# Side work of the experts one instruction per tile, thirteen conversions beside the attention, rows loaded ahead of the stores of y

## The chip, the core and the metric

The kernel runs on one core of one Trainium2 chip. The metric is device time in microseconds (us), the median of several executions. One execution was profiled on the hardware; all rows below come from that one.

The engines have short names: PE is TensorE (PEld its weight loads), DVE is VectorE, ACT is ScalarE, POOL is GpSimd and SP is SyncE, which issues most DMA transfers. Each engine works through its own queue in order; semaphores order the engines among each other.

## The reference

```python
scores = matmul(z, z.T) / S                  # B = 4, S = 3072, 64 wide
out = u * matmul(maximum(scores, 0) ** 2, v)  # 256 wide
x = out.reshape(B * S, 256)                   # 12288 tokens in one list
expert_idx = argmax(x @ w_gate, axis=1)       # 8 experts, capacity 384 each
h = maximum(disp @ w1[e], 0); y = h @ w2[e]   # 256 -> 1024 -> 256, scaled by the gate
h = y @ w_in; g = h * sigmoid(h)              # 256 -> 2048
result = g @ w_out                            # 2048 -> 256
```

An expert takes the first 384 tokens that choose it; tokens beyond that give zero rows. Tokens are attended in order until every expert is full, so that the kernel computes one whole batch of queries and 384 more, and branches to further code only if an expert still has room. Every product is done as three products of a head (fp32r) and a remainder, to keep the precision of float32.

## The kernel before, in words

**Attention.** Queries come in chunks: six of 512 and one of 384. A chunk goes over 24 key tiles of 128. One tick of the stream `st` is one tile: `scores` (two matmuls into a ps_s bank, relu on ACT, square on DVE), `square` of the tile before (head `ah` on ACT, remainder `al` on DVE) and `values` of the tile three before (six matmuls). Everything else is put into ticks with `st.at(t, f)`, and within a tick it stands in the order in which it was put there: loads and splits of z and v, clearing of DRAM, each chunk's routing (`route`, nine ticks after a chunk's last tile, with small DVE instructions and four scatters on POOL), and the *conversions*.

**Conversions.** w_in and w_out come as 64-bit floats. A `Convert` turns 512 columns into head and remainder, in seven steps: ACT makes two scaled copies (L199, L200), DVE does bit operations (L202, L205, L207, L210), ACT copies the head, and a product, a subtraction and an addition follow (L214, L215, L217), on POOL in the attention and on DVE in a late one. There are 16. The first `CV_N` are spread over the attention's free ticks (`free`, from `CV_A` to `TL + CV_B`, from the `CV_OFF`-th tick behind a chunk's end on); the words are loaded five ticks ahead. The rest are *late*: they are done beside the experts.

**Experts.** Eight units follow, one expert each with 384 tokens. Unit 0 runs at the end of the attention's stream, then the branch (L929), then units 1 to 7. `inward(i, tick)` does unit i: `hidden` for eight tiles (6 matmuls each into one of four ps_a banks, relu on ACT, remainder on DVE, L614), with this unit's w2 split beside the first four (head on ACT, remainder on POOL, L563), then `expert_out` (twice 24 matmuls into ps_s, a copy, a store of y), with the next unit's w1 split, its transposes and `split_x` (L601 on ACT, L602 on DVE) beside it. `tick` is called behind every tile of `hidden` and at eight places of `expert_out`. SP loads, in the program's order: the next expert's index (`look_up`), w1, the next unit's rows `xg` from `disp` (L584, `load`), w2, and the two stores of y (L631).

**Side work.** Beside units 1 to 6 each tick takes the next step of `work`: the late conversions, and then `Blocks.steps`, which makes four sums of blocks of w_in in two halves (`put` is a head on ACT, then a remainder on DVE). The words of a late conversion have one tile (`ut`), and the next are loaded inside the conversion before. What is left of `work` is drained ahead of unit 7.

**The end.** `quad` and `Pair` do w_in, the sigmoid and w_out in blocks, TensorE bound, to the end of the kernel.

Of the kernel before, what the change touches and what calls it, by code (L numbers as in the profile page):

```python
# [11 lines left out]
I32 = mybir.dt.int32  # L12
# [8 lines left out]
P = 128  # L21


def raw(ap):
    return ap.bitcast(F32)
# [3 lines left out]
def attention_moe_swish_kernel(  # L29
# [16 lines left out]
    E, _, F = w1.shape  # L46
# [9 lines left out]
    NTM = QC // P  # L56
# [107 lines left out]


    CW = 512
    CV_OPS, CV_OFF, CV_A, CV_B = 7, 6, 26, -14
    CV_N = 10

    class Convert:  # L170
        def __init__(self, i, src, hi, lo):
            self.src, self.hi, self.lo = src, hi, lo
            self.late = i > CV_N
            self.rw = rawt[NR + i % 2].bitcast(I32)

        def load(self):
            if self.late:
                self.rw = pools["ut"].tile([P, 2 * CW], I32, tag="ut", name="words")
            rv = self.rw
            if len(self.hi.shape) == 3:  # L180
                rv = rv.rearrange("p (a b) -> p a b", a=self.hi.shape[1])
            nc.sync.dma_start(out=rv, in_=self.src)

        def steps(self):
            t0 = pools["cv"].tile([P, CW], I32, tag="c0", name="c0")
            t1 = pools["cv"].tile([P, CW], I32, tag="c1", name="c1")
            t2 = pools["cv"].tile([P, CW], F32, tag="c2", name="c2")
            w = self.rw.rearrange("p (n two) -> p n two", two=2)
            hw, lw = w[:, :, 1], w[:, :, 0].bitcast(U32)
            f0, f1, f2 = t0.bitcast(F32), t1.bitcast(F32), t2  # L190
            hi, lo = self.hi, self.lo
            g0, g1, g2 = f0, f1, f2
            if len(hi.shape) == 3:
                g0, g1, g2 = (x.rearrange("p (a b) -> p a b", a=hi.shape[1]) for x in (f0, f1, f2))
            V = nc.vector

            nc.scalar.activation(f0, w.bitcast(F32)[:, :, 1], AF.Abs, scale=2.0 ** -16)  # L199
            nc.scalar.mul(f2, lw, 2.0 ** -52)  # L200
            yield
            V.tensor_scalar(f0, f0, 2.0 ** -31, None, ALU.max)  # L202
            yield

            V.tensor_scalar(t0, t0, 4, 1, ALU.logical_shift_left, ALU.logical_shift_right)  # L205
            yield
            V.scalar_tensor_tensor(t0, hw, -0x80000000, t0, ALU.bitwise_and, ALU.bitwise_or)  # L207
            yield

            V.tensor_scalar(t1, t0, -0x800000, None, ALU.bitwise_and)  # L210
            head(nc.scalar, hi, g0)
            yield
            eng = V if self.late else nc.gpsimd
            eng.tensor_tensor(f1, f1, f2, op=ALU.mult)  # L214
            eng.tensor_sub(g0, g0, raw(hi))  # L215
            yield
            eng.tensor_tensor(lo, g0, g1, op=ALU.add)  # L217
            yield
# [422 lines left out]
    class Blocks:  # L641
# [15 lines left out]
        def steps(self):  # L657
            self.s3 = self.s3()
            V = nc.vector
            tmp = lambda n: pools["el"].tile([P, QC], F32, tag="a", name=n, bufs=3)  # L660

            def put(to, x):
                nc.scalar.copy(to[0], x)
                V.tensor_sub(to[1], x, raw(to[0]))

            for c in range(HF // 512):
                (a11h, a11l), (a12h, a12l), (a21h, a21l), (a22h, a22l) = (
                    [raw(x) for x in a[c]] for a in (self.a11, self.a12, self.a21, self.a22))
                x, y = tmp("x"), tmp("y")
                V.tensor_add(x, a21h, a22h)  # L670
                V.tensor_add(y, a21l, a22l)
                yield
                V.tensor_add(x, x, y)
                yield
                put(self.s1[c], x)
                yield
                z = tmp("z")
                V.tensor_sub(z, x, a11h)
                V.tensor_sub(z, z, a11l)
                yield  # L680
                put(self.s2[c], z)
                yield
                x, y = tmp("x"), tmp("y")
                V.tensor_sub(x, a11h, a21h)
                V.tensor_sub(y, a11l, a21l)
                yield
                V.tensor_add(x, x, y)
                yield
                put(self.s3[c], x)
                yield  # L690
                V.tensor_sub(y, a12h, z)
                V.tensor_add(y, y, a12l)
                yield
                put(self.s4[c], y)
                yield

    class Slots:

# [167 lines left out]
    def inward(i, tick, split=True):  # L866

        u = units[i]
        nxt = units[i + 1] if i + 1 < len(units) else None
        new = nxt and nxt.x is not u.x  # L870
        w2s = u.x.split_w2() if split and not u.s0 else []
        if new:
            nxt.x.look_up()
            nxt.x.load_w1()
        if nxt and i:
            nxt.load()
        for f in range(FT):
            u.hidden(f)
            if w2s:
                w2s.pop(0)()  # L880
            tick()
        if new:
            nxt.x.load_w2()
        side = nxt.x.split_w1() if new else []
        side = [[f] for f in side] + [[] for _ in range(FT - len(side))]
        if nxt and i:
            side[0] += [nxt.keep_ids, lambda: nxt.transposes(0)]
            side[1] += [lambda: nxt.split_x(0), lambda: nxt.transposes(1)]
            side[2] += [lambda: nxt.split_x(1)]

        def beside():
            for f in side.pop(0):
                f()
            tick()

        for d in range(NH):
            u.expert_out(d, beside)
# [2 lines left out]
    tc.mark_branch_hint_location("full", "LikelyTaken", engines=tuple(  # L900
        getattr(mybir.EngineType, n) for n in ("PE", "DVE", "Activation", "Pool", "SP")))
    if early:
        inward(0, st.tick, False)
    st.finish()
    if early:
        units[1].load()


    def unless_full(label=None):
# [59 lines left out]

    def work():  # L970

        if late:
            late[0].load()
        for n, cv in enumerate(late):
            for k, _ in enumerate(cv.steps()):
                if k == 4 and n + 1 < len(late):
                    late[n + 1].load()
                yield
        yield from blocks.steps()

    work = work()
# [6 lines left out]
    nc.scalar.activation(pools["sm"].tile([1, 1], F32, tag="m", name="m"), warm[0:1, 0:1], AF.Sigmoid)  # L988
    for i in range(first, len(units)):
        if i + 1 < len(units):  # L990
            inward(i, lambda: next(work, None))
        else:
            for _ in work:
                pass
# [2 lines left out]
            slots[0].load()  # L997
            n = [0]

            def prepare():  # L1000
                n[0] += 1
                if n[0] == FT:

                    raws = [wts.tile([P, GK * D], F32R, tag=f"rawt{k}", name=f"part{k}") for k in range(4)]
                    sets[0] = halves(raws) + halves(big[0:3])
                    slots[0].parts = sets[0]
                    prepare.it = slots[0].steps()
                if n[0] > FT:
                    for _ in range(2):
                        next(prepare.it, None)  # L1010
# [185 lines left out]
```

## Time and profile before

| what | value |
|---|---|
| median of 3 runs | 770.39 us (769.28 to 770.55) |
| the profiled execution | 770.27 us, its span 768.2 us |
| attention and unit 0 | from 0 to 336.4 us of the span |
| branch and units 1 to 7 | from 336.4 to 498.5 us |
| the rest | from 498.5 to 768.2 us |

The span is the time from the first to the last instruction of the core. A row of a timeline begins with its start in the span and its duration; idle time ahead of it stands in brackets with the instruction that ended it. A row of windows gives a stretch, its length, the busy time (and the number of instructions) of PE, PEld, DVE, ACT and POOL, the granted clock of TensorE as a share of full speed, the busy share of the DMA engines and what they moved in GB/s.

### The profile page before, as it was taken

Reading aid. Unit: us, or ns where it says so; the run is one execution under the profiler, and the core shown is the slowest. Engines: PE = TensorE matmul, PEld = TensorE weight load, DVE = VectorE, ACT = ScalarE, POOL = GpSimd, SP = SyncE. Lnnn points to the kernel's source line nnn. Section 1 sums busy time; section 2 is a strip of 40 time slices with the busy share of each in tenths; the row PEclk is TensorE's granted clock in tenths of the full one; section 3 lists DMA queues with packets and bytes.
Section 4 is the critical chain, followed back from the end, with each engine's and each line's share of the span. In section 5 each row is a group of like instructions: output and inputs, shape, how many; then the busy total and the mean of one; then the engine's idle time right before and its main releaser. Section 6 shows DMA issues by size and latency. Waiting matters only on the chain.

```text
span 768.2 us, 11355 instructions
## 1 busy us (share of the span) xinstructions
PE 727.2 (95%) x3951; PEld 644.0 (84%) x3951; DVE 535.8 (70%) x964; ACT 499.2 (65%) x986; POOL 250.2 (33%) x237
## 2 busy tenths in 40 slices
PE   8999999999999999978878879989999999999995
PEld 6888887888888889978878879979999999999884
DVE  6778777787786867615887952578766876766770
ACT  6668777787777888735544455576566665565761
POOL 8622406233061882444563565200003100040004
PEclk9999999999999999989989899999999999999999
DMA  5815425052361423524641444121000000010001
GB/s 177 278 72 168 148 55 193 1 180 96 119 225 43 139 92 127 158 90 145 207 159 57 141 153 162 67 87 29 15 1 30 26 2 0 1 55 1 1 1 55
DMA packets 50668, 72.18 MB, mean 94 GB/s; under 512 B 3446, under 2 KB 38684, under 8 KB 50608
## 3 DMA queue, kind: packets, MB, share of 16 engines
q1 hardware_dynamic: 48160, 65.03, 26.6%
q0 software_dynamic: 2448, 6.39, 2.3%
q8 instruction: 32, 0.52, 0.3%
q14 instruction: 28, 0.23, 0.1%
HBM read 46.05 MB, written 25.77 MB: 93 GB/s over the span
## 4 chain that ended last, share of the span: by engine, by line
PE 39%; DVE 8%; ACT 3%; DMA 2%; issue 1%; SPq 0%; POOL 0%; POOLq 0%; ACTq 0%
PE ps_s L760 16%; PE ps_s L237 5%; PE ps_a L1029 5%; PE ps_a L1030 5%; PE ps_a L1031 4%; PE ps_a L237 3%; DMA words<-in_w_out 2%; DMA xg<-disp 1%; DVE c L215 1%; ACT big L1051 1%; DVE big L614 0%; DVE sg L1042 0%; PE ps_a L595 0%; POOL out L771 0%; DVE c L214 0%
## 5 line engine op out<-in xcount | busy, mean ns | idle before, releaser
L237 PE MATMUL ps_a<-ah,big 128*128 128x512 f32 (+1 forms) x672 | 183.0, 388 | 0.6 <-ACT ah L355 0.6
L237 PEld LDWEIGHTS ps_a<-ah,big 128*128 128x128 f32 x672 | 124.1, 188 | 21.5 <-POOL big L298 1.0
L342 ACT ACTIVATE r<-ps_s 128x512 f32<-128x512 f32 (+1 forms) x168 | 98.2, 585 | 57.3 <-PE ps_s L237 53.4
L356 DVE TENSOR_TENSOR al<-ps_s,ah 128x512 fp32r<-128x512 f32 (+1 forms) x168 | 111.6, 664 | 30.8 <-ACT ah L355 30.8
L347 DVE TENSOR_TENSOR ps_s<-ps_s,r 128x512 f32<-128x512 f32 (+1 forms) x132 | 89.4, 678 | 40.8 <-ACT r L342 40.2
L563 POOL TENSOR_TENSOR big<-rawt,big 128x512 fp32r<-128x512 f32 x64 | 88.6, 1406 | 77.2 <-ACT big L161 56.2
L760 PEld LDWEIGHTS ps_s<-wo,big 128*128 128x128 f32 x792 | 103.3, 190 | 7.7 <-ACT rows L768 2.7
L760 PE MATMUL ps_s<-wo,big 128*128 128x256 f32 x792 | 105.9, 283 | 1.8 <-ACT rows L768 1.8
L771 POOL DMA_INDIRECT out<-rows,ids x24 | 25.4, 1059 | 248.5 <-ACT rows L768 243.9
L237 PE MATMUL ps_s<-qt,kz 128*128 128x512 f32 (+1 forms) x336 | 104.8, 388 | 0.3 <-POOL kz L292 0.2
L237 PE MATMUL ps_a<-al,big 128*128 128x512 f32 (+1 forms) x336 | 101.3, 382 | 1.8 <-DVE al L356 1.7
L355 ACT CAST ah<-ps_s 128x512 fp32r<-128x512 f32 (+1 forms) x168 | 95.6, 569 | 3.3 <-DVE ps_s L347 3.1
L237 PE MATMUL ps_a<-qt,big 128*128 128x384 f32 x336 | 71.5, 373 | 18.4 <-DVE big L614 18.1
L237 PEld LDWEIGHTS ps_a<-qt,big 128*128 128x128 f32 x336 | 66.5, 213 | 22.1 <-DVE big L614 21.0
L237 PEld LDWEIGHTS ps_a<-al,big 128*128 128x128 f32 x336 | 62.6, 188 | 13.9 <-DVE al L356 2.6
L237 PEld LDWEIGHTS ps_s<-qt,kz 128*128 128x128 f32 x336 | 62.8, 188 | 11.9 <-POOL kz L292 0.7
L161 ACT CAST big<-rawt 128x512 fp32r<-128x512 f32 x86 | 51.6, 623 | 0.0
L460 POOL DMA_INDIRECT disp<-xr,idx x27 | 27.1, 1002 | 75.3 <-ACT ah L355 57.4
L1052 DVE TENSOR_TENSOR big<-sg,big 128x512 fp32r<-128x512 f32 x66 | 45.3, 688 | 7.1 <-ACT big L1051 5.9
L1042 DVE TENSOR_TENSOR sg<-ps_a,sg 128x512 f32<-128x512 f32 x72 | 48.0, 686 | 2.8 <-ACT sg L1041 0.7
L1051 ACT CAST big<-sg 128x512 fp32r<-128x512 f32 x66 | 41.0, 622 | 11.1 <-DVE sg L1042 11.1
L760 PEld LDWEIGHTS ps_s<-wo,late_c 128*128 128x128 f32 x348 | 45.9, 189 | 2.6
(227 smaller groups left out, 1249.8 us busy)
## 6 DMA issues: line engine op xcount, KB each, us to landing
rawt<-in_w SPq DMA_DIRECT2D x32, 512.0 KB, 4.6
out<-zero SPq DMA_DIRECT2D x16, 768.0 KB, 6.9
rawt<-in_v SPq DMA_DIRECT2D x11, 512.0 KB, 4.2
rawt<-in_w_in SPq DMA_DIRECT2D x8, 512.0 KB, 4.6
disp<-empty SPq DMA_DIRECT2D x6, 528.0 KB, 7.1
xg<-disp SPq DMA_DIRECT2D x8, 396.0 KB, 5.4
zr<-in_zT SPq DMA_DIRECT2D x12, 256.0 KB, 3.9
ut<-in_uT SPq DMA_DIRECT2D x6, 512.0 KB, 4.7
```

Of the source, the lines that this page charges most:

```text
L161: eng.copy(hi, x)
L237: nc.tensor.matmul(*a, **k)
L342: nc.scalar.activation(r[:, :Q], s[:, :Q], AF.Relu)
L347: nc.vector.tensor_mul(s[:, :Q], s[:, :Q], r[:, :Q])
L355: nc.scalar.copy(ah[:, :Q], a[:, :Q])
L356: nc.vector.tensor_sub(al[:, :Q], a[:, :Q], raw(ah[:, :Q]))
L563: nc.gpsimd.tensor_sub(ls[q][:, cs], rawt[r0 + q][:, cs], raw(hs[q][:, cs])))
L760: nc.tensor.matmul(o, lhsT=w[:, cs], rhs=wo[:, f, c:c + D], start=m not in self.seen, stop=last and n == 2, skip_group_check=True)
L1029: nc.tensor.matmul(ps, lhsT=ah, rhs=th, start=start, stop=False, skip_group_check=True)
L1042: nc.vector.tensor_mul(sg, src, sg)
L1051: nc.scalar.copy(gh, g)
L1052: nc.vector.tensor_sub(gl, g, raw(gh))
```

## The change

The late conversions become three: `CV_N` is 13, and their ticks run from 14 to `TL - 4`, from the ninth tick behind a chunk's end. Late words lie in two tiles by turns (`ut` and `xr`), two are loaded at the first step of the side work, and the load after next follows a whole conversion. Steps of the side work are cut to about one DVE instruction each, with `put` in two steps, and are called only behind tiles 5 to 7 of `hidden` and at seven of the eight places of `expert_out`. The next unit's rows are loaded ahead of w1, and unit 1's rows ahead of unit 0's stores of y instead of behind them.

```diff
-    CV_OPS, CV_OFF, CV_A, CV_B = 7, 6, 26, -14
-    CV_N = 10
+    CV_OPS, CV_OFF, CV_A, CV_B = 7, 9, 14, -4
+    CV_N = 13
...
-            self.late = i > CV_N
+            self.late, self.n = i > CV_N, i
...
             if self.late:
-                self.rw = pools["ut"].tile([P, 2 * CW], I32, tag="ut", name="words")
+                name, n = [("ut", 2 * CW), ("xr", NTM * ROW)][self.n % 2]
+                self.rw = pools[{"ut": "ut", "xr": "xr"}[name]].tile([P, n], I32, tag=name, name="words")[:, :2 * CW]
...
             eng.tensor_tensor(f1, f1, f2, op=ALU.mult)
+            if self.late:
+                yield
             eng.tensor_sub(g0, g0, raw(hi))
...
             def put(to, x):
                 nc.scalar.copy(to[0], x)
+                yield
                 V.tensor_sub(to[1], x, raw(to[0]))
+                yield
...
                 V.tensor_add(x, a21h, a22h)
+                yield
                 V.tensor_add(y, a21l, a22l)
                 yield
                 V.tensor_add(x, x, y)
-                yield
-                put(self.s1[c], x)
                 yield
                 z = tmp("z")
                 V.tensor_sub(z, x, a11h)
+                yield
+                yield from put(self.s1[c], x)
                 V.tensor_sub(z, z, a11l)
-                yield
-                put(self.s2[c], z)
                 yield
                 x, y = tmp("x"), tmp("y")
                 V.tensor_sub(x, a11h, a21h)
+                yield
+                yield from put(self.s2[c], z)
                 V.tensor_sub(y, a11l, a21l)
                 yield
                 V.tensor_add(x, x, y)
                 yield
-                put(self.s3[c], x)
-                yield
-                V.tensor_sub(y, a12h, z)
-                V.tensor_add(y, y, a12l)
-                yield
-                put(self.s4[c], y)
-                yield
+                V.tensor_sub(z, a12h, z)
+                yield
+                yield from put(self.s3[c], x)
+                V.tensor_add(z, z, a12l)
+                yield
+                yield from put(self.s4[c], z)
...
         if new:
             nxt.x.look_up()
-            nxt.x.load_w1()
         if nxt and i:
             nxt.load()
+        if new:
+            nxt.x.load_w1()
         for f in range(FT):
             u.hidden(f)
             if w2s:
                 w2s.pop(0)()
-            tick()
+            tick(f)
         if new:
             nxt.x.load_w2()
+        if early and not i:
+            nxt.load()
...
-            tick()
+            tick(2 * FT - 1 - len(side))
...
     if early:
-        inward(0, st.tick, False)
+        inward(0, lambda f: st.tick(), False)
     st.finish()
-    if early:
-        units[1].load()
...
-        if late:
-            late[0].load()
+        for cv in late[:2]:
+            cv.load()
         for n, cv in enumerate(late):
-            for k, _ in enumerate(cv.steps()):
-                if k == 4 and n + 1 < len(late):
-                    late[n + 1].load()
-                yield
+            for _ in cv.steps():
+                yield
+            if n + 2 < len(late):
+                late[n + 2].load()
         yield from blocks.steps()
...
-            inward(i, lambda: next(work, None))
+
+            inward(i, lambda f: next(work, None) if f > 4 and f != FT else None)
```

## Rows read from the trace of the kernel before

**Rows 1.** Waits of PE, 300 to 505 us: in total, times, longest.

```profile
PE ps_a L237 <- DVE big L614: 18.1, 8, 4.6
PE ps_a L595 <- SPq L929: 4.9, 1, 4.9
```

**Rows 2.** Windows: the branch, units 1, 4, 6 and 7, and all eight stretches.

```profile
336.39:342.77 6.38, 1.45 (x8) 1.15 (x7) 0.02 (x1) 0.96 (x2) 0.19 (x1) 0.68 0.33 97
342.77:366.42 23.65, 20.28 (x104) 19.73 (x104) 13.90 (x23) 13.77 (x28) 9.99 (x8) 0.87 0.45 151
...
414.88:442.34 27.46, 21.05 (x103) 20.25 (x103) 24.41 (x32) 12.05 (x25) 12.76 (x10) 0.88 0.30 99
...
464.36:481.86 17.50, 17.50 (x103) 17.18 (x103) 5.58 (x10) 9.95 (x20) 10.21 (x9) 1.00 0.50 166
481.86:498.53 16.67, 16.67 (x98) 16.67 (x97) 9.35 (x16) 9.72 (x19) 5.05 (x4) 1.00 0.22 76
sum 162.14, PE 137.40 PEld 131.28 DVE 103.72 ACT 82.39 POOL 75.24; mean PE 17.17 PEld 16.41 DVE 12.96 ACT 10.30 POOL 9.41
```

**Rows 3.** Timeline, unit 1: the first words and what follows them.

```profile
350.61 0.66 ACT L199 ACTIVATE c<-words 128x512 f32<-128x512 f32 x1 [4.43 <-DMA words<-in_w_out]
...
352.84 4.69 PE L237 MATMUL ps_a<-qt,big 128*128 128x384 f32 x18 [3.37 <-DVE big L614]
```

**Rows 4.** Timeline, start of unit 3.

```profile
390.35 1.77 DVE L215 TENSOR_TENSOR c<-c,wo 128x512 f32<-128x512 f32 x1
...
392.88 0.66 ACT L199 ACTIVATE c<-words 128x512 f32<-128x512 f32 x1 [3.10 <-DVE wo L217]
...
395.71 1.53 PE L237 MATMUL ps_a<-qt,big 128*128 128x384 f32 x6 [2.50 <-DVE big L614]
```

**Rows 5.** Groups by line, 340 to 500 us: first and last conversion line of seven.

```profile
L215 DVE TENSOR_TENSOR c<-c,wo 128x512 f32<-128x512 f32 x6 | 8.4, 1408 | 0.0
...
L202 DVE TENSOR_SCALAR c<-c 128x512 f32<-128x512 f32 x6 | 2.5, 422 | 1.7 <-ACT c L199 1.7
```

**Rows 6.** Timeline, unit 6, which has no side work.

```profile
464.36 8.48 PE L237 MATMUL ps_a<-qt,big 128*128 128x384 f32 x48
...
466.13 0.56 DVE L614 SCALAR_TENSOR_TENSOR big<-ps_a,big 128x384 fp32r<-128x384 f32 x1 [6.22 <-ACT big L613]
...
476.80 0.56 DVE L602 TENSOR_TENSOR qt<-ps_a,qt 128x384 fp32r<-128x384 f32 x1 [0.82 <-ACT qt L601]
```

**Rows 7.** Line L215, late conversions: ns, least, median and most.

```profile
L215 DVE TENSOR_TENSOR c<-c,wo x6: 679/1766/1784, 358.7 to 410.2; 128x512 f32<-128x512 f32 x6
```

**Rows 8.** Timeline at the branch.

```profile
337.60 0.39 SPq L584 DMA_DIRECT2D xg<-disp  x1
...
341.32 1.51 PE L595 MATMUL ps_a<-ident,xg 128*128 128x128 f32 x6 [4.93 <-SPq L929]
```

**Rows 9.** Line L929, the branch: first and last start on SP.

```profile
L929 SPq EVENT_SEMAPHORE  x9: 17/17/17, 339.2 to 341.2; - x9
```

**Rows 10.** DMA issues, 318 to 345 us: KB each, us to landing.

```profile
yT<-y SPq DMA_DIRECT2D x2, 192.0 KB, 2.0
```

**Rows 11.** Timeline, routing of chunk 1 beside chunk 2.

```profile
115.15 1.22 DVE L455 TENSOR_TENSOR sl<-sl,base 128x4 f32<-128x4 f32 x1
...
118.98 0.30 PEld L237 LDWEIGHTS ps_a<-al,big 128*128 128x128 f32 x2 [2.17 <-DVE al L356]
```

**Rows 12.** Timeline, end of chunk 0.

```profile
39.97 0.62 POOL L159 TENSOR_SCALAR qt<-zq 128x512 fp32r<-128x512 f32 x1 [3.36 <-DMA zq<-in_zT]
...
41.93 2.55 POOL L298 TENSOR_TENSOR big<-rawt,big 128x512 fp32r<-128x512 f32 x2
...
44.63 1.07 PE L237 MATMUL ps_a<-ah,big 128*128 128x512 f32 x4
```

**Rows 13.** Timeline of POOL: a conversion's product in the attention.

```profile
251.25 1.30 POOL L214 TENSOR_TENSOR c<-c,c 128x512 f32<-128x512 f32 x1
```

**Rows 14.** Windows of 10 us, columns as in rows 2.

```profile
30.00:40.00 10.00, 10.00 (x46) 8.29 (x45) 6.94 (x11) 7.60 (x15) 4.45 (x5) 1.00 1.08 357
```

More of the change, by code (lines that the diff above doesn't have):

```diff
@@ L998, in attention_moe_swish_kernel, with prepare @@
             n = [0]
-            def prepare():
+            def prepare(f):
                 n[0] += 1
```

## The prediction

> **What bounds the kernel now.** I read the waits of TensorE first. Between 300 and 505 us it waits for almost one thing only: `hidden` (L237, ps_a) waits for the DVE subtraction L614, 18.1 us in 8 waits, and once for the branch (L929), 4.9 us [rows 1]. So the attention is bound by TensorE itself, and the part where something is to be had is the seven expert units behind the branch. Second, the busy times by unit, cut where the 48 matmuls of `hidden` begin [rows 2]. Unit 6, without any side work, takes 17.50 us and TensorE is busy in all of them; unit 7 takes 16.67. Unit 1 takes 23.65, unit 4 takes 27.46. Units 1 to 7 together take 162.14 - 6.38 = 155.76 us. Seven clean ones would take 6 x 17.50 + 16.67 = 121.67. So **34.1 us** are stall, all of it in units 1 to 5, and DVE is busy there in 24.41 of 27.46 us in unit 4, against 5.58 of 17.50 in unit 6.
>
> Third, the order of time around two of the stalls. In unit 1 the first step of the side work sits behind tile 0: ACT's L199 stands 4.43 us waiting for the words of w_out, the relu of the next tile is queued behind it, and TensorE runs out of banks [rows 3]. In unit 3 the steps from the unit before still fill DVE: L215 takes 1.77 us, ACT waits 3.10 us for DVE before L199, and the subtraction of tile 0 that TensorE needs comes so late that it stands for 2.50 us [rows 4]. TensorE always stops after 24 matmuls, that is after four tiles, because ps_a has four banks.
>
> **The expert units.** The side work now is one DVE instruction per step, behind tiles 5 to 7 and seven of the eight places of the output: 10 steps per unit, 60 in units 1 to 6. The work is 3 conversions x 8 steps and 2 x 18 steps of the blocks, 60 as well, so nothing is left for the drain before unit 7. Three conversions leave. Six cost 39.6 us of DVE here (seven lines of six instructions, from 8.4 us for L215 down to 2.5 for L202) [rows 5], so three take 19.8. DVE in units 1 to 5 was 103.72 - 0.02 - 5.58 - 9.35 = 88.8 us, less 5 x 5.58 for the units' own work 60.9; 41.1 remain, spread over six units: 6.9 + 5.58 = 12.4 us in 17.5. The throughput fits.
>
> Then the latency, on the clean unit 6 [rows 6]. Its start is 464.36; the subtraction of tile 0 ends 2.3 us later, that of the second split_x 13.0 us later (476.80 + 0.56). Six steps follow on DVE before the next unit's tile 0. At the mean of a step, 41.1/49 = 0.84 us (3 x 7 + 2 x 14 = 49 of the 60 steps have a DVE instruction), five of them take 4.2 us and end at 17.2; TensorE needs tile 0's bank back only after four tiles, at 17.5 + 8.48/2 = 21.7. The cover is about 4 us; without it each microsecond of lateness costs one. The three steps behind tiles 5 to 7 delay hl of the last tiles, which the output reads last: tile 5's subtraction starts at 1.77 + 5 x 1.04 = 7.0, and even with a step of 1.78 us [rows 7] behind it and behind tile 6's, tile 7's ends at 7.0 + 3 x 0.56 + 2 x 1.78 = 12.2; it is wanted at 8.5 + 22 x 0.174 = 12.3. The ACT copies (`put`) now have a step between them and the subtraction, so DVE no longer stands for them. The first words are loaded at the first step, behind tile 5: SP reaches that load about where it does now, ACT about 6 us later, which covers the 4.43 us. With two tiles (ut, xr) the next words are there a conversion ahead. Nothing stands that I can see: 34.1 us go. From 0 to 16 us of stall may remain (the upper end is the second rival); I take 2, because the mean of a step is nearer to the undisturbed 0.68 than to 1.78.
>
> A rule that speaks against this. Steps of DVE that read SBUF meet GpSimd's L563: L215 takes from 0.68 to 1.78 us [rows 7]. The Trainium skill (SBUF — State Buffer, Who interferes with whom) says that a DVE instruction with two SBUF inputs and a GpSimd instruction that reads SBUF exclude each other for the whole instruction. By that rule every step that meets one could pay the full 1.78; the trace shows both ends, so it agrees. With each step at that price the sum would be rival 1's, with the mean it is the forecast's.
>
> **The branch.** The load of unit 1's rows (L584) is issued at 337.60, behind the last store of y, and TensorE starts at 341.32 [rows 8]. SP's semaphores behind the branch run from 339.2 to 341.2: it waits there for its own transfers [rows 9]. With the rows loaded before the stores only the last yT is awaited, issued at about 336.9 and landed 2.0 us later [rows 10]: 339.0, and I estimate 0.5 us for the rest of the semaphores. TensorE starts at 339.6, **1.7 us** earlier (bounds: 0, if the store is as late as the rows; 2.4, without its wait). It still restarts at the lower of its two levels: in unit 1 the mean clock was 0.87 [rows 2], so 0.13/0.5 x 23.65 = 6.1 us were at 1.2 GHz, in two spells. One of the two goes with the wait for the words; the other, 3 us at half speed, costs 1.5 us over the clean unit. Behind the branch the rows' load goes ahead of w1 on SP, so w1 lands 0.5 us later; it is wanted only in the output.
>
> **The attention.** 13 conversions instead of 10, 91 steps in 76 free tiles instead of 70 in 70: fifteen tiles get two. DVE and ACT have the room on average (three conversions are about 6 us each on either over 270 us). Two places change.
> (a) At 115 us small DVE instructions of the routing meet a conversion on GpSimd (L455: 1.22 us) and TensorE's next weight load stands 2.17 us for `al` [rows 11]. The new offset 9 starts conversions after the routing: **-2.1 us** (0 to 2.2).
> (b) The first conversion now lies in tiles 14 to 19. On GpSimd its L214 and L215 stand between chunk 1's split (39.97, after a wait of 3.36 us for zq) and the split of the last v (41.93, 2.55 us for two halves), whose first half the second matmul of the run at 44.63 wants, at about 44.85 [rows 12]. It ends at 43.2 now. L214 and L215 add 2.6 us (1.30 each [rows 13]), and the second conversion's words, 512 KB, are queued ahead of zq while the transfers run at 357 GB/s [rows 14]: 1.5 us. 43.2 + 2.6 + 1.5 = 47.3: TensorE stands **2.5 us** (0 to 4).
> The last two conversions meet GpSimd's splits of batch 1 (250 to 288 us); I put 0.3 us there (0 to 3).
>
> **Sum.** Against the profiled execution's own 770.27 us (span 768.2; median of the runs 770.39, so the two can be used alike): -34.1 + 1.5 + 2.0 - 1.7 - 2.1 + 2.5 + 0.3 = -31.6, **738.7 us**. The other ends: without (b), without what remains and without the low clock 732; what follows is for the top.
>
> **Rivals.**
> 1. *The lock with GpSimd decides.* All steps pay 1.78: 8.2 DVE steps per unit are 14.6 + 5.6 = 20.2 us in 17.5, 2.7 us per unit, 16 in six, in place of my 2: 753 us. For: half of L215's instructions here take that long. Against: behind tiles 0 to 4 there are no steps, and that is when GpSimd splits w2; only the first steps of the output meet w1's splits. Chance 0.12.
> 2. *Attention gives some back.* (b) at 4 us, and the last conversion's four DVE steps at 1.78 in 7.2 us, 3 us of stall in place of 0.3: +4 to +6, 743 to 745. Chance 0.13.
> 3. *The doubled tiles stall.* If each of the fifteen tiles with two steps stops TensorE, at the 2.17 us of the stall at 119 us they cost 32.6 and the time is 771; from 31.6/15 = 2.1 us each on the kernel is slower than before (2.5: 776). Against: ten conversions cost one such stall now, and that one met the routing. Chance 0.03.
> 4. *The side work isn't done in its places*, is drained before unit 7 and costs there what it did: about 770. The count, 60 in 60, speaks against it: 0.01.
>
> **Chances.** The forecast, 733 to 742, has 0.71, the rivals 0.12, 0.13, 0.03 and 0.01. Range 732 to 752: it takes in rival 2 and most of what lies toward rival 1. About 0.2% is what a measurement of this kernel tells from no change: faster 0.96, same 0.01, slower 0.03.
>
> **What would show it.** Units 1 to 6 at 17.5 to 18.5 us from `hidden` to `hidden`; no wait of TensorE for L614; ACT's waits for words gone or in unit 1 alone; TensorE behind the branch at about 3.2 us after its last matmul instead of 4.9; no wait for `al` near 119 us; but a wait of TensorE for GpSimd's L298 near 45 us. It is wrong if L614 of tile 0 still comes over 4 us after the unit's start, which means that DVE isn't through with the last steps, or if new waits for `al` appear where tiles have two steps.

## The result and the profile after

The changed kernel takes **738.4 us** (median of 4 runs, 737.6 to 740.5), the kernel before on the same chip 770.0: ratio 0.959, 95% interval 0.957 to 0.962, so 4.1% faster. The prediction was 738.7, its range 732 to 752. The profiled execution took 737.7 us, its span is 735.9.

The waits of TensorE, whole span (in total, times, longest). The lines of the changed kernel have moved: `hidden` is L240 (L237 before), its DVE subtraction L617 (L614), the branch L935 (L929), a conversion's product, subtraction and addition L215, L218 and L220 (L214, L215, L217). Against [rows 1], L617 is gone from the list, the wait at the branch has halved, and two waits of the attention are new in it.

```profile
PE ps_a L598 <- SPq L935: 2.5, 1, 2.5
PE ps_a L240 <- POOL big L301: 2.4, 1, 2.4
...
PE ps_a L240 <- DVE al L359: 1.2, 1, 1.2
```

Busy time by unit, as in [rows 2]: the branch, then units 1, 4, 6 and 7.

```profile
338.50:342.89 4.39, 1.62 (x11) 1.08 (x10) 0.02 (x1) 1.01 (x3) 0.59 (x2) 1.00 0.15 55
342.89:362.21 19.32, 19.32 (x102) 18.89 (x103) 12.85 (x19) 12.76 (x25) 11.00 (x9) 0.91 0.63 207
396.96:414.33 17.37, 17.37 (x103) 17.25 (x103) 12.87 (x19) 11.44 (x23) 11.63 (x9) 1.00 0.52 169
431.70:449.08 17.38, 17.38 (x104) 17.26 (x103) 12.72 (x18) 11.05 (x23) 12.12 (x9) 1.00 0.50 168
449.08:465.74 16.66, 16.66 (x97) 16.66 (x97) 9.98 (x17) 10.16 (x20) 5.06 (x4) 1.00 0.23 76
```

Unit 4 went from 27.46 to 17.37 us, and DVE does 12.87 us in it where it did 24.41. TensorE is busy in all of a unit that has side work. Unit 1 is 2 us longer than the others, without a wait: its mean clock is 0.91.

The waits are only part of what went. By [rows 2], TensorE was busy for 137.40 - 1.45 = 135.95 of the 155.76 us of units 1 to 7 before, where clean units need 121.67. So 19.8 us of the 34.1 were idle time, and 14.3 us were matmuls that took longer, 13.7 of them in units 1 to 4, where the granted clock was 0.87, 0.92, 0.80 and 0.88. Unit 3 shows it:

```profile
388.88:414.88 26.00, 22.14 (x103) 20.68 (x103) 21.61 (x29) 13.16 (x28) 13.47 (x10) 0.80 0.47 157
```

In the changed kernel, where TensorE doesn't stop, it is 1.00 in units 2 to 7: the clock came back where the waits ended. (Not every wait had lowered it: unit 5 of before had waits and a clock of 1.00.)

The timeline of unit 4 shows how. The output's last steps still run on DVE, and two of them are long; but they are through before tile 0 of the next unit (414.33) needs its subtraction.

```profile
396.96 8.48 PE L240 MATMUL ps_a<-qt,big 128*128 128x384 f32 x48
398.78 0.56 DVE L617 SCALAR_TENSOR_TENSOR big<-ps_a,big 128x384 fp32r<-128x384 f32 x1 [0.56 <-ACT big L616]
...
410.89 1.67 DVE L693 TENSOR_TENSOR x<-x,y 128x512 f32<-128x512 f32 x1
412.48 1.78 DVE L695 TENSOR_TENSOR z<-wih,z 128x512 f32<-128x512 f32 x1
...
414.33 0.86 PE L240 MATMUL ps_a<-qt,big 128*128 128x384 f32 x4
```

Tile 0's L617 ends 2.4 us after the unit's start, as in the unit without side work [rows 6]; all 48 matmuls of `hidden` run without a gap.

In unit 1 the words' wait of [rows 3], 4.43 us, is 0.28:

```profile
344.94 1.00 SPq L183 DMA_DIRECT2D words<-in_w_out  x2
...
352.02 0.67 ACT L200 ACTIVATE c<-words 128x512 f32<-128x512 f32 x1 [0.28 <-DMA words<-in_w_out]
```

The attention gives a little back. At the end of chunk 0, beside [rows 12]:

```profile
43.24 1.49 POOL L215 TENSOR_TENSOR c<-c,c 128x512 f32<-128x512 f32 x1
...
44.23 0.61 PE L240 MATMUL ps_s<-qt,kz 128*128 128x512 f32 x2
...
44.70 1.54 POOL L218 TENSOR_TENSOR c<-c,wih 128x512 f32<-128x512 f32 x1
...
46.20 2.96 POOL L301 TENSOR_TENSOR big<-rawt,big 128x512 fp32r<-128x512 f32 x2
...
47.51 0.96 PE L240 MATMUL ps_a<-ah,big 128*128 128x512 f32 x3 [2.44 <-POOL big L301]
...
48.78 0.62 PE L240 MATMUL ps_s<-qt,kz 128*128 128x512 f32 x2
```

Two conversion instructions of GpSimd, L215 and L218, stand ahead of the split of the last v (L301), and TensorE waits for it: the tile that begins at 44.23 lasts 4.55 us where an undisturbed tile lasts 1.81 (2.74 more). The other place is at 265 to 272 us, in the second batch:

```profile
264.92 3.39 DVE L206 TENSOR_SCALAR c<-c 128x512 int32<-128x512 int32 x1
265.44 1.33 POOL L215 TENSOR_TENSOR c<-c,c 128x512 f32<-128x512 f32 x1
...
266.68 1.33 POOL L218 TENSOR_TENSOR c<-c,wo 128x512 f32<-128x512 f32 x1
...
268.23 0.69 DVE L350 TENSOR_TENSOR ps_s<-ps_s,r 128x512 f32<-128x512 f32 x1
...
269.56 0.73 PE L240 MATMUL ps_a<-al,big 128*128 128x512 f32 x2 [1.16 <-DVE al L359]
```

L206, a DVE step of a conversion whose median is 0.43 us, takes 3.39. The attention's own L350 stands behind it, `al` comes late, and two tiles last 3.25 and 2.25 us, 1.9 more than two clean ones. The wait for `al` near 119 us [rows 11] is gone.

The account below is worked out from the starts of matmuls in the two traces: the first and last tile of the attention, `hidden` of each unit, the first matmul of the part behind unit 7.

| stretch | before | after | change | predicted |
|---|---|---|---|---|
| attention, first tile to last tile | 307.92 | 310.69 | +2.8 | +0.7 |
| last tile to unit 1 | 30.44 | 27.74 | -2.7 | -1.7 |
| units 1 to 7 | 155.76 | 122.85 | -32.9 | -30.6 |
| from there to the end | 269.72 | 270.13 | +0.4 | 0 |

That is -32.4, of -32.6 between the two profiled executions (770.27 and 737.7); the rest lies outside the span.

### The profile page after: what moved, and what is told of

It is laid out like the page before. It is cut to its first block, busy times and chain, and to the rows that moved or that the text cites. A ratio compares the mean times of both kernels' runs of the same rounds, so it can differ in the third digit from the quotient of the medians.

```text
span 735.9 us, 11357 instructions
## 1 busy us (share of the span) xinstructions
PE 714.8 (97%) x3951; PEld 635.3 (86%) x3951; DVE 525.4 (71%) x955; ACT 502.8 (68%) x986; POOL 265.9 (36%) x246
## 4 chain that ended last, share of the span: by engine, by line
PE 48%; ACT 2%; DVE 1%; issue 1%; POOL 0%; POOLq 0%; ACTq 0%
PE ps_s L765 17%; PE ps_a L240 8%; PE ps_s L240 8%; PE ps_a L1036 5%; PE ps_a L1037 5%; PE ps_a L1038 5%; PE ps_a L598 1%; ACT big L1058 1%; DVE sg L1049 0%; POOL out L776 0%; DVE ps_a L1080 0%; ACT u L1079 0%; ACT u L1095 0%; ACT sg L1048 0%; ACT u L1105 0%
## 5 line engine op out<-in xcount | busy, mean ns | idle before, releaser
L240 PE MATMUL ps_a<-ah,big 128*128 128x512 f32 (+1 forms) x672 | 183.3, 389 | 3.0 <-POOL big L301 2.4
L240 PEld LDWEIGHTS ps_a<-ah,big 128*128 128x128 f32 x672 | 123.9, 188 | 24.5 <-POOL big L301 3.9
L350 DVE TENSOR_TENSOR ps_s<-ps_s,r 128x512 f32<-128x512 f32 (+1 forms) x132 | 89.3, 677 | 38.1 <-ACT r L345 36.6
L566 POOL TENSOR_TENSOR big<-rawt,big 128x512 fp32r<-128x512 f32 x64 | 90.3, 1436 | 43.0 <-ACT big L161 38.0
L240 PE MATMUL ps_s<-qt,kz 128*128 128x512 f32 (+1 forms) x336 | 105.3, 390 | 0.0
L240 PE MATMUL ps_a<-al,big 128*128 128x512 f32 (+1 forms) x336 | 101.5, 383 | 1.3 <-DVE al L359 1.2
L240 PEld LDWEIGHTS ps_a<-al,big 128*128 128x128 f32 x336 | 62.4, 188 | 13.9 <-DVE al L359 2.6
L240 PEld LDWEIGHTS ps_s<-qt,kz 128*128 128x128 f32 x336 | 63.0, 189 | 11.3 <-POOL kz L295 0.4
L240 PE MATMUL ps_a<-qt,big 128*128 128x384 f32 x336 | 61.3, 341 | 0.2 <-ACT qt L604 0.2
L240 PEld LDWEIGHTS ps_a<-qt,big 128*128 128x128 f32 x336 | 59.8, 192 | 0.8 <-ACT qt L604 0.5
L161 ACT CAST big<-rawt 128x512 fp32r<-128x512 f32 x86 | 51.4, 621 | 0.5 <-DMA rawt<-in_v 0.3
```

The source lines that it names most:

```text
L161: eng.copy(hi, x)
L240: nc.tensor.matmul(*a, **k)
L350: nc.vector.tensor_mul(s[:, :Q], s[:, :Q], r[:, :Q])
L566: nc.gpsimd.tensor_sub(ls[q][:, cs], rawt[r0 + q][:, cs], raw(hs[q][:, cs])))
```

## The experiments

No kernel here leaves out a part of the computation. The ratio is that to the kernel before on the same chip (three chips: medians 772.9, 772.75 and 770.5 us), and the stretches are those of the table above, from one profiled execution each. They are set side by side first, since several experiments are read against the same rows.

| kernel | ratio, 95% interval | attention | units 1 to 7 |
|---|---|---|---|
| before | 1 | 307.9 | 155.8 |
| changed | 0.959 (0.957 to 0.962) | 310.7 | 122.9 |
| changed_again | 0.960 (0.958 to 0.962) | 312.0 | 122.6 |
| rows_behind | 0.962 (0.960 to 0.965) | 313.5 | 122.4 |
| start_20 | 0.956 (0.954 to 0.958) | 310.8 | 122.9 |
| end_14 | 0.955 (0.953 to 0.957) | 309.7 | 121.9 |
| start_20_end_14 | 0.958 (0.956 to 0.960) | 312.8 | 122.6 |
| off_6 | 0.956 (0.954 to 0.958) | 310.2 | 122.2 |
| one_tile | 0.959 (0.957 to 0.961) | 312.3 | 122.7 |
| all_ticks | 0.973 (0.970 to 0.975) | 311.0 | 133.1 |
| coarse | 0.972 (0.968 to 0.975) | 313.7 | 129.9 |
| ten | 0.970 (0.968 to 0.972) | 306.8 | 134.9 |
| twelve_15 | 0.956 (0.955 to 0.958) | 309.3 | 123.6 |
| eleven_15 | 0.963 (0.961 to 0.965) | 308.6 | 130.5 |

Six of these executions (changed, changed_again, rows_behind, one_tile, all_ticks, coarse) place the conversions of the attention alike, and their attention still lasts from 310.7 to 313.7 us: the stall near 45 us costs 2.7 to 4.0 in them. A difference of a microsecond or two in that column says little alone.

**The rows behind the stores again.**

```diff
-        if early and not i:
-            nxt.load()
...
     st.finish()
+    if early:
+        units[1].load()
```

> The changed kernel, but unit 1's rows are loaded behind unit 0's stores of y again, as before the change. Theory (SP's wait for its own transfers sets the restart behind the branch): TensorE's wait there goes back from 2.5 us to 4.9 us, the time is 2.4 to 2.7 us above the changed kernel's 738.4, so about 741, and nothing else moves. Rival (the stores of y alone would hold the restart, the rows are hidden anyway): under 0.5 us.

The wait of TensorE:

```profile
PE ps_a L598 <- SPq L935: 4.9, 1, 4.9
```

It is that of before, 2.4 us more than in the changed kernel, and from the last tile to unit 1 the kernel takes 30.4 us, as before (27.7 in the changed one). By ratio it loses 0.3% (0.962 against 0.959), 2.3 us, with intervals that overlap. The gain at the branch comes from the rows' place.

**Where the first and the last conversion of the attention stand.** Three kernels with other bounds for the ticks:

```diff
-    CV_OPS, CV_OFF, CV_A, CV_B = 7, 9, 14, -4
+    CV_OPS, CV_OFF, CV_A, CV_B = 7, 9, 20, -4    # start_20
+    CV_OPS, CV_OFF, CV_A, CV_B = 7, 9, 14, -14   # end_14
+    CV_OPS, CV_OFF, CV_A, CV_B = 7, 9, 20, -14   # start_20_end_14
```

> The changed kernel with the first conversion at tile 20 instead of 14, so that its three GpSimd instructions stand behind the split of the last v; 91 steps lie in 70 tiles, 21 of them with two. Theory (the stall of 2.4 us near 45 us is GpSimd's order plus zq's delay): the wait for L301 falls to at most 0.3 us, since v's first half is done at about 44.6 and wanted at 44.9; the time falls by 2.4 to 2.7 us to about 735.8. Rival (tiles with two steps stall TensorE): new waits for the remainder al, no gain. Second rival (zq alone does it): over 1 us of the wait stays.

> The changed kernel with the last conversion ended at tile 120 instead of 139, out of the stretch in which GpSimd splits batch 1; 24 tiles have two steps. The first conversion's L215 and L218 come one tile earlier and can run while GpSimd waits for zq. Theory: the stall at 267 to 272 us (1.9 us over two tiles) goes; near 45 us only L220's 1.3 us stand ahead of the split of v, so that the wait there falls from 2.4 to about 1.2 us; together -3.0 us, about 735.4. Rival (the last stall comes from the splits and the routing alone, as the 0.3 us of the kernel before did): the stall stays, -1.2 us.

> Both shifts: conversions from tile 20 to tile 120 alone, 91 steps in 61 tiles, 30 of them with two steps. Theory (stalls come from where GpSimd's instructions meet the routing, the splits of v or the splits of batch 1, not from two steps in a tile): both stalls go, the attention takes what its matmuls take, -4.3 us, about 734.1. Rival (density stalls TensorE): thirty tiles with two steps cost more than the two stalls gave, 738 or above.

In start_20 the wait for L301 is gone; chunk 0 takes 41.59 us against 44.32 in the changed kernel and 41.58 before. So the first conversion made it. But the late stall grew to three tiles of 3.51, 3.69 and 2.67 us, and the profiled attention is no shorter. By ratio the kernel is 2.8 us faster than the changed one (0.956 against 0.959), about what was expected, but the intervals overlap and the profile doesn't show where. The timeline of start_20 there:

```profile
263.51 3.02 DVE L203 TENSOR_SCALAR c<-c 128x512 f32<-128x512 f32 x1
263.69 1.32 POOL L215 TENSOR_TENSOR c<-c,c 128x512 f32<-128x512 f32 x1
...
264.93 1.31 POOL L218 TENSOR_TENSOR c<-c,wo 128x512 f32<-128x512 f32 x1
...
267.79 0.73 PE L240 MATMUL ps_a<-al,big 128*128 128x512 f32 x2 [1.42 <-DVE al L359]
```

It is another line of the conversion that takes 3 us, L203, but again one that meets L215 and L218 of GpSimd. In end_14 the late stall is gone, as expected: no tile between 254 and 280 us lasts over 1.9 us. The wait for L301 is down to 0.9 us. New stalls of 0.5 to 1 us appear in tiles 115 and 121, and the profiled attention is 1.0 us shorter, not 3. By ratio it does gain what was expected, 3.6 us with intervals that don't overlap (0.9547 against 0.9594). The profiles place 1.0 us of it in the attention and 1.0 in unit 1, whose clock was 0.95; the rest they don't place. With both edits the two stalls are gone and tiles 25, 49, 73, 97 and 121 last 2.1 to 2.9 us: TensorE waits there for `ah` (3.1 us in 5 waits), since ACT has the conversion's copy L161 ahead of it, which stands 2.0 us for DVE's L208. So neither place need stall; thirteen conversions pushed into fewer tiles stall a little in many. That was the rival in the expectation, and it has the case: the attention takes 312.8 us, and by ratio the kernel is level with the changed one.

**The offset back at 6.**

```diff
-    CV_OPS, CV_OFF, CV_A, CV_B = 7, 9, 14, -4
+    CV_OPS, CV_OFF, CV_A, CV_B = 7, 6, 14, -4
```

> The changed kernel with conversions from the sixth tile behind a chunk's end on, as before the change: 91 steps in 91 tiles, none with two. Theory (GpSimd's conversion instructions slow the routing's small DVE instructions): stalls of about 2 us each where GpSimd's steps fall on the routing, at tiles 33 to 36 and 82 to 85, and the stall near 45 us gone, because the first conversion's GpSimd steps fall behind the split of v and the second's words behind zq; the stall near 268 us stays. Together +1 to +2 us. Rival (two steps in a tile make the stalls): with none left, all stalls go, -4 us.

The routing does meet a conversion again, in two places, and in one of them, in chunk 3, TensorE stalls (tile 84 lasts 3.56 us):

```profile
159.91 1.12 DVE L457 TENSOR_SCALAR dr<-sl 128x4 f32<-128x4 f32 x1
...
160.96 1.30 POOL L218 TENSOR_TENSOR c<-c,wih 128x512 f32<-128x512 f32 x1
161.06 1.21 DVE L458 TENSOR_TENSOR sl<-sl,base 128x4 f32<-128x4 f32 x1
...
162.33 1.29 POOL L220 TENSOR_TENSOR wil<-c,c 128x512 fp32r<-128x512 f32 x1
162.38 1.26 DVE L470 COPY count<-count 128x8 bf16<-128x8 bf16 x1
```

Three instructions on 128x4 or 128x8 elements take 1.1 to 1.3 us each; the same kind, undisturbed, takes 0.16 to 0.19 a moment before and after. This is the mechanism of term (a). But the whole isn't slower: with this offset the conversions miss the end of chunk 0 and nearly miss the late place, and by ratio it is level with start_20. It has another stall, in tile 146 at 280.8 us (3.43 us), where ACT stands 2.7 us for a transfer of v ahead of the copy that TensorE wants. The expectation that offset 9 is the better one, by 1 to 2 us, isn't borne out: it takes away one stall and brings two.

**The units: places, size and number of the steps.** First the steps behind all 16 places instead of ten:

```diff
-            inward(i, lambda f: next(work, None) if f > 4 and f != FT else None)
+            inward(i, lambda f: next(work, None))
```

> The changed kernel, but the side work is called at all sixteen places of a unit again instead of ten; it is then done in units 1 to 4. Theory (the five free tiles let DVE catch up before TensorE needs a bank): the first words are awaited at tile 0 of unit 1, 3 to 5 us; in units 2 to 4 sixteen steps of 0.84 us and 5.6 us of own work are 17.4 to 19 us of DVE in 17.4, so 0 to 1.5 us each; together 4 to 9 us above 738.4. Rival (the gain came from three conversions less and the second words' tile, the places are free): under 1 us. The waits of TensorE for L617 tell which.

Units 1 to 6 take 26.5, 17.9, 18.1, 19.2, 17.4 and 17.4 us. Unit 1 has most of it:

```profile
352.61 0.66 ACT L200 ACTIVATE c<-words 128x512 f32<-128x512 f32 x1 [5.76 <-DMA words<-in_w_out]
354.23 0.56 DVE L617 SCALAR_TENSOR_TENSOR big<-ps_a,big 128x384 fp32r<-128x384 f32 x1 [7.22 <-ACT big L616]
...
354.84 2.61 PE L240 MATMUL ps_a<-qt,big 128*128 128x384 f32 x7 [4.14 <-DVE big L617]
```

That is [rows 3] again. The words are no later than in the changed kernel; ACT reaches them 5.5 us earlier and stands, with the relus queued behind. Starting behind tile 5 covers this. The loss, 10.2 us in the units, is over the 4 to 9 expected. Units 2 to 4 lose 3.1 of it, as expected; unit 1 loses 7.2 where 3 to 5 were expected, 4.1 in the wait above and some 3 with its clock, which is 0.81 (0.91 in the changed kernel).

Next the steps of before, two DVE instructions or a copy and its remainder in one, in the new places (the conversion's product and subtraction in one step, `put` without a yield, the blocks' sums paired as before):

```diff
             eng.tensor_tensor(f1, f1, f2, op=ALU.mult)
-            if self.late:
-                yield
             eng.tensor_sub(g0, g0, raw(hi))
...
                 nc.scalar.copy(to[0], x)
-                yield
                 V.tensor_sub(to[1], x, raw(to[0]))
-                yield
```

> The changed kernel with the steps of the kernel before (two or three instructions in some, the head's copy and the remainder in one step): 41 steps instead of 60 at the same ten places per unit. Theory (short steps keep DVE from standing for ACT's copy and from running late): a unit's ten steps take about 11.3 us of DVE and some 2 us of waits for ACT, with 5.6 of its own over 17.4, so 1 to 2 us of stall in each of four units: 3 to 8 us above 738.4. Rival (only the places matter): under 1 us.

Units 1 to 3 take 18.7, 17.4 and 17.4 us; units 4 and 5, at whose starts the blocks' steps of the unit before are still running, 22.0 and 20.5. The start of unit 4 (line numbers are lower by two here):

```profile
404.10 1.80 DVE L693 TENSOR_TENSOR y<-y,wil 128x512 f32<-128x512 f32 x1
405.83 1.94 DVE L615 SCALAR_TENSOR_TENSOR big<-ps_a,big 128x384 fp32r<-128x384 f32 x4
406.43 5.68 PEld L238 LDWEIGHTS ps_a<-qt,big 128*128 128x128 f32 x24 [3.09 <-DVE big L615]
```

`hidden` begins at 399.33, and DVE is still in the block's steps: the first of them and the copy between keep it until 405.83, 6.5 us later, and then the subtractions come four at once. Small steps are needed, but only for the blocks' sums, which alternate with ACT. Two units pay 3.1 and 4.6 us where four were expected to pay 1 to 2 each; the 7.0 us together lie in the expected 3 to 8, the whole by ratio, 9 us, above it.

Third, ten conversions in the attention as before, six late ones (84 steps for 60 places):

```diff
-    CV_N = 13
+    CV_N = 10
```

> The changed kernel with ten conversions in the attention and six late ones: 48 + 36 = 84 steps for 60 places, so 24 steps are drained ahead of unit 7. Theory: 24 steps are 17 to 20 us of DVE, of which TensorE hides four tiles, 4.2 us: 13 to 16 us above, less up to 2 us of stall in the attention: 750 to 754. Rival (the number of late conversions matters little, since their DVE work was never the limit): under 3 us.

With thirteen conversions placed as in the changed kernel the attention takes 2.8 to 5.8 us more than before, in six profiled executions. With ten in the new places it is shorter than before, 306.8 against 307.9. But units 1 to 6 aren't disturbed either (18.2 us in unit 1, 17.4 in the others); what has no place is drained before unit 7, which takes 29.7 us instead of 16.7:

```profile
PE ps_a L240 <- DVE big L617: 10.8, 1, 10.8
```

The other 2.3 us of unit 7's 13.0 go with its clock, 0.83. By ratio the kernel is 8 us above the changed one, where 12 to 16 were expected: the attention is 3.9 us shorter than the changed kernel's, not up to 2.

Last, one tile for the words instead of two, loaded inside the conversion before, as it was:

```diff
-                name, n = [("ut", 2 * CW), ("xr", NTM * ROW)][self.n % 2]
+                name, n = ("ut", 2 * CW)
...
-        for cv in late[:2]:
-            cv.load()
+        if late:
+            late[0].load()
```

> The changed kernel with one tile for the late words, the next loaded inside the conversion before, as it was before the change; the places and the short steps stay. Theory (the wait for words mattered because it came ahead of tile 0's relu): ACT waits up to 2 us for the second and third words, at the last places of a unit, and TensorE sees nothing of it: within 0.5 us of the changed kernel. Rival (the second tile is what took away the waits): 3 us or more above, with TensorE waiting for L617 behind the words.

Units 1 to 6 take 19.1 and five times 17.4: the second tile isn't needed here.

**A version between.** If thirteen conversions are too many for the attention and ten too many for the units, twelve or eleven, with more places behind the tiles of `hidden` and all eight of the output, may do better:

```diff
-    CV_OPS, CV_OFF, CV_A, CV_B = 7, 9, 14, -4
-    CV_N = 13
+    CV_OPS, CV_OFF, CV_A, CV_B = 7, 9, 15, -4
+    CV_N = 12                                                      # eleven_15: 11
...
-            inward(i, lambda f: next(work, None) if f > 4 and f != FT else None)
+            inward(i, lambda f: next(work, None) if f > 3 else None)   # eleven_15: f > 2
```

> Twelve conversions beside the attention, from tile 15 on (84 steps in 75 tiles, nine with two), four late ones, and the side work called behind tiles 4 to 7 and at all eight places of the output: 32 + 36 = 68 steps in 72 places. Theory (stalls of the attention come from GpSimd's steps in bad places, and the units have room on DVE: 53 us of side work over six units and 5.6 us of own work are 14.4 in 17.4): no stall over 1 us in the attention, units 2 to 6 stay at 17.4 us; 3.5 to 4.5 us less than the changed kernel on the same chip. Rival (the units are full at ten steps): the units lengthen by 0.5 to 2 us each, no gain.

> Eleven conversions beside the attention from tile 15 on (77 steps in 75 tiles), five late ones, the side work behind tiles 3 to 7 and at all eight places of the output: 40 + 36 = 76 steps in 78 places. Theory: the attention runs without a stall, as it did with ten conversions; the units need about 60 us of side work, 15.5 of 17.4 us of DVE, so 0 to 1 us of stall each: between 4.5 us less and 1 us more than the changed kernel. Rival (three free tiles are too few): TensorE waits for L617 in each unit, over 1 us each.

> The changed kernel itself once more, so that the next kernels can be set beside it on one chip: 0.96 of the kernel before.

twelve_15 takes 736.65 us where the changed kernel takes 740.17 on the same chip, ratios 0.956 (0.955 to 0.958) and 0.960 (0.958 to 0.962): 3.5 us less, as expected. By ratio end_14, start_20 and off_6 are level with it. Its attention, 2.7 us shorter, has no stall at 265 to 272 us and none over about 1 us elsewhere; unit 1 is 1.3 us shorter, with a clock of 1.00 in this execution; units 2 to 4 pay 0.7 to 0.8 us each for four late conversions, as the rival in the expectation has it, but that doesn't take up the gain. Units 1 and 2:

```profile
341.37:359.13 17.76, 17.76 (x103) 17.33 (x103) 10.51 (x18) 12.25 (x25) 10.43 (x9) 1.00 0.60 206
359.13:377.31 18.18, 17.64 (x103) 17.20 (x103) 14.00 (x21) 11.79 (x25) 11.53 (x10) 1.00 0.62 213
```

eleven_15 is slower than the changed kernel, 742.5 us, by 0.3% with intervals that just touch: with steps behind tiles 3 and 4 as well, units 1 and 3 take 19.9 and 21.1, part of it at a clock of 0.91 and 0.92. Against twelve_15, one conversion fewer in the attention was worth 0.8 us there, and that conversion and the further place cost 6.9 in the units.

## Why the prediction was right, and where its terms were off

**The units' stall, -34.1, and what remains of it, +2.0.** Right in the sum, and a little too cautious: no wait of TensorE for L617 is left, so what remains is nothing, and the low clock in unit 1 costs 1.9 against the 17.4 of the others, with 1.5 forecast. A unit now takes 17.37 where the clean one took 17.50, 0.8 us in six. DVE has 12.9 us of work in unit 4, with 12.4 forecast from the average; by the same working a step takes 0.87 us at the mean (76.1 us of DVE in units 1 to 6, less 6 x 5.58, over 49), with 0.84 forecast. The 4 us of cover on which the sum rested are confirmed from the other side: in coarse DVE comes to tile 0 at 6.5 us, and TensorE stands 2.8 us at the start of units 4 and 5 each.

Two readings behind the term were too simple. It calls all 34.1 us stall, with the clock in unit 1 alone; but 14.3 of them were matmuls that took longer, nearly all in units 1 to 4 at a lower clock, and they went as the clock came back where the waits ended. And TensorE doesn't always stop after 24 matmuls: in unit 1 of before it did so after 30, since 18 are left in [rows 3].

The undo experiments give back 10 us (places), 7 (step size) and 12 (number of late conversions) of the units' 33, and none (second tile). They don't add up to 33, and needn't: DVE's lateness below the cover is free, so one part undone costs only what goes past it, and what the clock falls with it. No single one of these parts makes the gain. The order of the rows' load ahead of w1 in the units was not undone; no run shows its share.

**Rival 1, the lock with GpSimd.** It doesn't decide the units. Single steps do pay its price, 1.67 and 1.78 us for L693 and L695 above, which run beside GpSimd's splits (L566). The Trainium skill (SBUF — State Buffer, Who interferes with whom) says that a DVE instruction with two SBUF inputs contends with a GpSimd instruction that reads SBUF; the trace agrees. But L685 and L688, at 404 to 406 us, where GpSimd is idle, take 0.68, and the mean of all stays inside the cover.

**The branch, -1.7: the term was too small.** Measured -2.7, 2.4 of it in the wait itself, past or at the bound of 2.4 that the prediction gave for no wait.

```profile
339.81 0.34 SPq L634 DMA_DIRECT2D yT<-y  x1
341.80 0.85 PE L598 MATMUL ps_a<-ident,xg 128*128 128x128 f32 x6 [2.53 <-SPq L935]
L935 SPq EVENT_SEMAPHORE  x9: 17/17/17, 341.3 to 342.0; - x9
```

The step that was off is that TensorE starts 0.5 us after the last yT has landed. It was issued at 339.81 and landed 2.1 us later, 341.91; TensorE started before that, at 341.80. SP's semaphores of L935 run over 0.7 us, where they took 2.0 [rows 9]. In ten and eleven_15 the wait is 3.0 us, near the 3.2 forecast, and TensorE does start behind the landing there, by 0.4 us (in ten 338.33 against 337.95); why it goes one way or the other stays open. The remaining 0.4 us is the clock: the prediction has TensorE restart at the lower level, but here the clock is 1.00 up to 342.89, and the six transposes take 0.85 us where they took 1.51 [rows 8]; it falls in unit 1. In end_14 they take 1.51 again, so this part is luck of the execution.

**(a), -2.1.** Right: the tile at 119 us is back at 1.81 us (-2.0), and off_6 shows the routing's small instructions at 1.1 to 1.3 us as soon as a conversion meets them.

**(b), +2.5.** Right in mechanism and size: +2.7 in the first profile, 2.7 to 4.0 over six executions. The split of zq starts 1.3 us later than before (41.29 against 39.97), with 1.5 forecast, and L215 and L218 take 3.0 with 2.6 forecast. start_20 takes the stall away.

**The last conversions, +0.3: mis-sized.** It is 1.9 us here, within the bound of 3. I took 1.78 us as the most that a DVE step can cost; the longest in the trace of before was 1.80. The row of after has 3.39, and start_20's 3.02. In both, the step begins 0.2 to 0.5 us ahead of the first of two GpSimd instructions back to back, beside the end of a scatter, and ends 0.3 us behind the end of the second. The Trainium skill (SBUF — State Buffer, Who interferes with whom) says that a `tensor_scalar` can run in a mode that takes both port pairs and can then contend with GpSimd. The trace agrees that the step is held up, but it stood past the end of L215 and through L218; whether it ran in that mode no row shows. end_14 removes the stall by moving these steps. That moving helps is shown; that it is the ports alone is argued from the two traces, and no run here isolates it.

**Rival 2** named the two places, and some executions have (b) at 4.0 us and the late stall at 1.9; but the late stall comes from one step of 3.39 us and not from four of 1.78, and its 743 to 745 us didn't come. That the total came out so near the forecast is in part luck: the attention's term was 2.1 too low, the branch's 1.0 and the units' 2.3 too high, and the part behind unit 7, put at nothing, took 0.4 more. (The terms that make the prediction's other end add up to 732.7, not 732.) **Rival 3** is refuted: by the kernel's bounds the doubled tiles are 14, 19, 24, 39, 44, 59, 64, 69, 84, 89, 94, 109, 114, 119 and 134, and none of them lasts over 0.2 us more than an undisturbed one; the stalls lie in tiles 23, 138 and 139, which have one step each. **Rival 4** is refuted by unit 7, 16.66 us; ten shows what it would have cost when the count is exceeded.

## What to carry to other kernels

Side work on an engine that feeds the bound engine is free as long as its lateness stays under the slack of the buffers between (here four banks, about 4 us): size its steps and choose its places by that, not by the average load. Count steps against places, because what doesn't fit comes out as one long wait at the end; and work moved elsewhere has to be followed there, where it may stall at a chunk's end. A wait that goes can take a low clock with it: read the busy time of the bound engine beside its waits, or the gain of ending them is counted short. A split between the two extremes was worth a run of its own: twelve conversions, with two more places in each unit, were 3.5 us faster than thirteen on the same chip, and eleven were slower.

## What was not expected of the hardware

A DVE TENSOR_SCALAR with one input of 128x512, 0.43 us at the median of 16, took 3.39 us beside GpSimd instructions back to back, nearly twice what any DVE instruction paid before (1.80). Instructions on 128x4 elements went from 0.18 to 1.2 us in the same company, as one had before the change [rows 11]. And the semaphores behind a branch took SP 2.0 us where it had issued the rows' load just before, and 0.7 where it had not.
